# Batch 0 through quadrant scores, a seven-product first stage in the last unit, and a new order of all steps

## The chip, the cores and the metric

The kernel runs on one core of a Trainium2 chip. The metric is the device time of one execution in microseconds (us); the median of several runs counts. One further execution was recorded by the hardware profiler, and all durations come from that one. The engines are PE (TensorE), DVE (VectorE), ACT (ScalarE), POOL (GpSimd) and SP (SyncE, which here only issues DMAs).

## What is computed

Eight batches of attention with pooled keys and values, followed by an MLP mixer over the 576 tokens and the 512 channels:

```python
def _attn_ref(q, k, v):                      # 8 batches, 8 heads, 576 tokens, 64 wide
    k_p = k.reshape(B, H, Sp, 8, D).mean(axis=3)     # 72 pooled keys
    v_p = v.reshape(B, H, Sp, 8, D).mean(axis=3)
    scores = scale * np.matmul(q, k_p.transpose(0, 1, 3, 2))
    attn = softmax(scores)
    return np.matmul(attn, v_p)

def _moe_ref(x, w_tok1, w_tok2, w_ch1, w_ch2):       # x: 8 x 576 x 512
    xt = x.transpose(0, 2, 1)
    h = np.maximum(xt @ w_tok1, 0.0) @ w_tok2        # 576 -> 256 -> 576
    u = x + h.transpose(0, 2, 1)
    h2 = np.maximum(u @ w_ch1, 0.0) @ w_ch2          # 512 -> 1536 -> 512
    return u + h2
```

(The lines are shortened; the softmax subtracts the row's maximum.) Inputs and output are fp32; the kernel multiplies in bf16 and adds up in fp32.

## The kernel before

**Units.** The channel MLP is cut into nine units of 512 rows: unit n (0 to 7) takes tokens 0 to 511 of batch n, and unit 8, the last, takes the remaining 64 tokens of all eight batches. The function `unit_fast` (L574) makes one unit. Its first stage has twelve tiles (`l1_tile`, L514): each is four matmuls of 512 columns with a weight of `w_ch1`, summed in one PSUM bank (L517), and one relu by ACT into the tile `GT` (L521). Its second stage is seven half products of twelve matmuls of 256 columns (L583), after Strassen's scheme in Winograd's form: DVE makes sums of parts of GT (`g_sums`, steps "=1" to "=4", L545 and L557, into the tile called area) and of `w_ch2` (`weight_sum`, steps w0 to w3, made once, area2), and adds up the products (L626, tiles s1, s5, s4, oa and ob, called s and o in the profile). In units 0 to 7 the products come in the order x, y, z, x again, w, z again, x again. In the last unit w is left out and the product is put behind as a seventh on x; x lies there in two PSUM tiles of `ps_two`, called p in the profile. A product that adds to a bank has to wait until DVE has read the bank's earlier state.

**Steps of a batch.** What turns q, k and v of a batch into a unit's input is a set of named steps (`batch_steps`, L187): loads (lk, lq, lv), pooling of k and v by eights (K0, K1, V0, V1 on POOL and k0, k1, v0, v1 on DVE, all by `pool8`, L171, three additions for half the heads; kpool and vpool0, vpool1 on PE, eight matmuls with the identity each), kpT (the pooled k transposed into kD), Q0 and Q1 (q transposed in 32 by 32 blocks by DVE into qD, L284), s0 to s2 (scores and exponentials), av0 to av4 (attention times values and division by the sum, L379 to L384), at0 and at1 (first token matmul and relu), u0 to u4 (second token matmul and residual, L415), t0 to t3 (transposition by PE) or M0 to M4, M, MT and T0 to T5 (the same through HBM, by SP's DMAs and DVE).

**Order.** The program order is written by hand. `HEAD` (L21) lists the steps before unit 0, and `PLAN` (L22) has one entry for each unit: after the unit's i-th piece (two matmuls of a first-stage tile, or four of a product), the steps under i are issued. Each engine runs its instructions in that order. The step g (`gate`, L711) makes POOL wait for what DVE has before it. Four single PSUM banks (p1a to p1d) are handed out in turn (`take`, `give`), and two double tiles (p) serve scores and attention.

**The head.** Batch 0 goes its own way. Two fp32 transfers by SP bring the first half of q (into qf, which lies in area2), cast by ACT and DVE (steps c0, c1); the other half, k and v come by POOL's converting transfers (`first_kv`, L130, parts A, B and T: first heads, second heads, last eight rows). q is transposed by PE (`qT`, five transposes a step, q0 to q3), k is pooled by PE (`kp2`, kp0 to kp2) and transposed by PE with zeros beside it (`kt2`), and each score step (o0 to o3, e0 to e3, L318) makes the scores of one pair of heads, odd or even tokens. Attention times values comes in halves of the heads (a00 to a14, L333), the token matmuls too (m00 to m14, L356), and the unit's input is made transposed at once (X0 to X3 and A0 to A3, L468 and L476). The steps d1, d2 and so on are spare matmuls on a zeroed tile, 19 in all (L679).

Of the kernel before, what the change touches and what calls it, by code (L numbers as in the profile page):

```python
# [8 lines left out]
FP32 = mybir.dt.float32  # L9
BF16 = mybir.dt.bfloat16  # L10
# [10 lines left out]
HEAD = """LkA LkT LkB LvT Lq LvA LvB Lt1 Lk1 Lt2 Lc1b Lc1a Lq1 Lc1c Lv1 Lc1d p1 Lc2a Lc2b Lc2c d2 d2 d3 d1 d4 d4 c0 c1 prep q0 kp0 kp1 kt0 q1 d1 o0 kt1 kp2 e0 e1 q3 kt2 o1 q2 e3 vpool0 o3 e2 a00 vpool1 a02 o2 m01 d1 d1 m00 a04 X1 m03 a14 m02 X0 m04 p0 a10 a12 1.kpool m10 m14 m12 m13 m11 A1 A0 X2 X3 A2 A3"""  # L21
PLAN = [  # L22
# [13 lines left out]
def kernel(  # L36
# [18 lines left out]
    BOUNCED = range(3, B)  # L55
    SP = S // POOL
    BP, BR = 64, S // 64
    NE = (BR + 1) // 2
    EV, OD = NE * BP, (BR - NE) * BP
# [35 lines left out]
    GT = singles.tile([P, NM, 4 * P], BF16)  # L95
    area2 = early.tile([P, 6 * 1024], BF16, name="area2")
    qf = area2[:, 0:4 * BR * D].bitcast(FP32).rearrange("p (a n) -> p a n", a=2)
    f2 = area2[:, 2304:2304 + 2 * S].rearrange("p (c n) -> p c n", c=2)
    warm = area2[:, 3584:4096]
    uT_tails = singles.tile([P, 4, 4 * P], BF16)  # L100
    u_tails = singles.tile([P, 2, DM, 2], BF16)
    area = early.tile([P, 6 * 1024], BF16, name="area")
    kpz = area[0:SP, 0:1536].rearrange("j (h e d) -> j h e d", h=H, e=3)
    kT = area[:, 2048:2048 + 2 * H * SP].rearrange("m (o k) -> m o k", o=2)
    qT0 = area[:, 3200:3200 + 2 * HP * EV].rearrange("m (a l n) -> m a l n", a=HP, l=2)
# [3 lines left out]
    exps = [singles.tile([SP, H * S + BP], BF16, name=f"ex{i}") for i in range(2)]  # L109
# [20 lines left out]
    def first_kv(key, part):  # L130
        if (0, key) not in loaded:
            loaded[0, key] = raw.tile([SP, H, POOL, D], BF16, name=key + "r")
        h0, h1, j0, j1 = {"A": (0, HP, 0, BP), "B": (HP, H, 0, BP), "T": (0, H, BP, SP)}[part]
        kv(loaded[0, key], k if key == "k" else v, 0, h0, h1, j0, j1)

    def q_pairs(a0, a1):
        return q[0, 2 * a0:2 * a1].rearrange("(a l) (p r) d -> (l p) a (r d)", l=2, r=BR)
# [49 lines left out]
    def batch_steps(b):  # L187
# [5 lines left out]
        def prepare():  # L193
            kp = att.tile([SP, 2, 2, 4, D // 2], BF16, name="kp") if b >= 1 else None
            st.update(kp=kp, vp=values[par], ex=exps[par], xt=rests[b // 2 % 2])
            if not first:
                st["kD"] = att.tile([P, 2, 2, SP], BF16, name="kD")
# [29 lines left out]
        def kp2(h0, h1):  # L227
            def go():
                ps = take([P, 512], FP32)
                n = (h1 - h0) * D  # L230
                for i in range(POOL):
                    nc.tensor.matmul(out=ps[0:SP, 0:n], lhsT=ident[0:SP, 0:SP], rhs=loaded[b, "k"][:, h0:h1, i, :],
                                     start=(i == 0), stop=(i == POOL - 1))
                nc.vector.tensor_copy(out=kpz[:, h0:h1, 1, :], in_=ps[0:SP, 0:n].rearrange("j (h d) -> j h d", d=D))
                give(ps)
            return go

        def kt2(h0, h1):
            def go():
                ps = take([P, 2, h1 - h0, SP], BF16)  # L240
                for odd in range(2):
                    for h in range(h0, h1):
                        nc.tensor.transpose(out=ps[:, odd, h - h0, :],
                                            in_=kpz[:, h, 1 - odd:3 - odd].rearrange("j e d -> j (e d)"),
                                            identity=ident[0:SP, 0:SP])
                nc.vector.tensor_copy(out=kT[:, :, h0 * SP:h1 * SP], in_=ps.rearrange("m o h j -> m o (h j)"))
                give(ps)
            return go
# [22 lines left out]
        def qT(hp):  # L271
            def go():
                ps = take([P, NE, 2, BP], BF16)
                for rr in range(NE):
                    nc.tensor.transpose(out=ps[:, rr].rearrange("m l p -> m (l p)"),
                                        in_=loaded[b, "q"][:, hp, rr * P:(rr + 1) * P], identity=ident)
                nc.vector.tensor_copy(out=qT0[:, hp].rearrange("m l (r p) -> m r l p", p=BP), in_=ps)
                give(ps)
            return go

# [8 lines left out]
        def scores(i):  # L289
            def go():  # L290
                pss = [ps_two.tile([P, 2, 512], FP32, name="p2") for _ in range(2)]
                spans = [(i, 0, 0, S1)] if i < 2 else [(g, g * (S - S1), S1, S) for g in range(2)]
                for g, o, n0, n1 in spans:
                    for db in range(2):
                        for l in range(4):
                            quad = slice(l * 32, (l + 1) * 32)
                            nc.tensor.matmul(out=pss[l // 2][0:SP, l % 2, o:o + n1 - n0], lhsT=st["kD"][quad, g, db, :],  # L297
# [3 lines left out]
                for a in range(2):  # L301
                    if i < 2:
                        dst, src = exv[:, a, :, i, 0:S1], pss[a][0:SP, :, 0:S1]
                    else:
                        dst, src = exv[:, a, :, :, S1:S], pss[a][0:SP, :, 0:2 * (S - S1)].rearrange("j l (g n) -> j l g n", g=2)
                    nc.scalar.activation(out=dst, in_=src, func=AF.Exp, scale=scale)  # L306
            return go

        def score(hp, odd):
            n = OD if odd else EV  # L310

            def go():
# [470 lines left out]
```

## Time and profile before

| | |
|---|---|
| Runs | 265.97 us median of 3 (265.03 to 266.37) |
| Profiled execution, span | 264.4 us |
| PE busy | 256.2 us, 2121 matmuls |
| DVE, ACT, POOL busy | 178.4, 119.6, 153.1 us |
| First matmul of unit 0, of unit 8 | 24.60 us, 240.72 us |
| Last unit: first product, last product | 251.09 us, 259.42 us |
| Granted clock of PE, mean | 0.999 |

The span runs from the first to the last instruction of the profiled execution; the time of a run also holds what lies around it. A matmul's row shows its whole passage, 0.379 us for 512 columns, while the next one starts 0.216 us after it, so that many matmuls in a row are read from their starts.

### The profile page before, as it was taken

How to read it: one execution, taken by the hardware profiler on the slowest of the kernel's cores; microseconds unless marked ns; L12 is line 12 of the kernel's file. 1: busy time of each engine (PE TensorE's matmuls, PEld its weight loads, DVE VectorE, ACT ScalarE, POOL GpSimd, SP SyncE). 2: the span in 40 equal slices, each digit the busy share in tenths (PEclk: the TensorE clock that was granted, in tenths of full speed). 3: DMA queues.
4: the chain of work that ended last, by engine and by line, in shares of the span. 5: the costliest groups of instructions: out<-in, count | busy, mean ns of one | idle time of the engine just before them, and what ended most of it. 6: DMA issues, size and time to landing. Idle time of an engine off the chain costs nothing.

```text
span 264.4 us, 5328 instructions
## 1 busy us (share of the span) xinstructions
PE 256.2 (97%) x2121; PEld 160.3 (61%) x2121; DVE 178.4 (67%) x370; ACT 119.6 (45%) x195; POOL 153.1 (58%) x177
## 2 busy tenths in 40 slices
PE   8799999989999999999999999999999999999994
PEld 3685466744677545774487447744874486486483
DVE  3557569996787655895599678844795576184183
ACT  2355763149536456425641575165435412612700
POOL 8577326899999999988959982898200010100000
PEclk9999999999999999999999999999999999999999
DMA  6999999993088928699447940830513053404104
GB/s 141 193 195 206 205 207 208 205 216 80 4 129 141 166 82 171 149 202 266 91 132 107 232 144 17 158 94 4 159 38 122 30 170 80 121 0 102 59 0 159
DMA packets 31704, 34.29 MB, mean 130 GB/s; under 512 B 3136, under 2 KB 23744, under 8 KB 31680
## 3 DMA queue, kind: packets, MB, share of 16 engines
q0 software_dynamic: 17632, 17.64, 42.3%
q1 hardware_dynamic: 13632, 15.93, 20.2%
q10 hardware_dynamic: 416, 0.39, 0.5%
q8 instruction: 16, 0.26, 0.4%
q14 instruction: 8, 0.07, 0.1%
HBM read 38.99 MB, written 12.58 MB: 195 GB/s over the span
## 4 chain that ended last, share of the span: by engine, by line
PE 73%; DVE 12%; POOL 8%; issue 3%; DMA 2%; ACT 1%; POOLq 0%; ACTq 0%
PE p1c L517 10%; PE p1b L517 8%; PE p1a L517 7%; PE p1d L517 7%; PE p1d L583 6%; PE p1c L583 5%; PE p1b L583 4%; PE p1a L583 4%; POOL t L174 3%; PE p L297 3%; DVE x L384 3%; DVE area L545 3%; PE p L379 2%; DMA kr<-in_k_dram 2%; POOL t L175 2%
## 5 line engine op out<-in xcount | busy, mean ns | idle before, releaser
L517 PEld LDWEIGHTS <-w_ch 128*128 128x128 bf16 x432 | 39.5, 98 | 44.4 <-issue 2.7
L713 POOL COPY flag<-flag 1x1 f32<-1x1 f32 x47 | 15.3, 326 | 86.0 <-DVE flag L712 86.0
L583 PEld LDWEIGHTS <-area 128*128 128x128 bf16 x432 | 41.4, 98 | 7.8 <-issue 1.2
L306 ACT ACTIVATE ex<-p 72x768 bf16<-72x768 f32 x42 | 31.6, 803 | 17.1 <-PE p L297 17.1
L583 PEld LDWEIGHTS <-GT 128*128 128x128 bf16 x324 | 30.7, 98 | 7.9 <-issue 1.6
L175 POOL TENSOR_TENSOR t<-t 72x512 f32<-72x512 f32 x23 | 31.2, 1358 | 1.8
L517 PE MATMUL p1c<-uT,w_ch 128*128 128x512 bf16 x116 | 31.4, 379 | 0.0
L521 ACT ACTIVATE GT<-p1b 128x512 bf16<-128x512 f32 x27 | 16.1, 597 | 27.5 <-PE p1b L517 20.9
L521 ACT ACTIVATE GT<-p1c 128x512 bf16<-128x512 f32 x32 | 19.1, 598 | 15.5 <-PE p1c L517 11.7
L517 PE MATMUL p1b<-uT,w_ch 128*128 128x512 bf16 x96 | 26.0, 379 | 0.0
L174 POOL TENSOR_TENSOR t<-kr 72x1024 f32<-72x1024 bf16 x12 | 25.5, 2121 | 0.4
L174 POOL TENSOR_TENSOR t<-vr 72x1024 f32<-72x1024 bf16 x11 | 23.4, 2125 | 1.0 <-DMA vr<-in_v_dram 0.5
L517 PE MATMUL p1a<-uT,w_ch 128*128 128x512 bf16 x88 | 23.9, 379 | 0.0
L517 PE MATMUL p1d<-uT,w_ch 128*128 128x512 bf16 x84 | 22.2, 379 | 0.0
L521 ACT ACTIVATE GT<-p1a 128x512 bf16<-128x512 f32 x25 | 14.9, 597 | 15.4 <-PE p1a L517 14.8
L521 ACT ACTIVATE GT<-p1d 128x512 bf16<-128x512 f32 x24 | 14.4, 599 | 12.8 <-PE p1d L517 7.3
L384 DVE TENSOR_TENSOR x<-p,den 128x512 bf16<-128x512 f32 x28 | 19.3, 691 | 1.0
L545 DVE TENSOR_TENSOR area<-GT 128x1536 bf16<-128x1536 bf16 x9 | 11.3, 1257 | 11.9 <-ACT GT L521 6.7
L557 DVE TENSOR_TENSOR area<-GT 128x1536 bf16<-128x1536 bf16 x9 | 9.5, 1054 | 11.3 <-ACT GT L521 11.3
L379 PEld LDWEIGHTS <-ex 72*128 72x128 bf16 x280 | 12.9, 98 | 6.5 <-DVE x L384 1.4
L379 PE MATMUL p<-vp,ex 72*128 72x65 bf16 x280 | 14.4, 194 | 0.3 <-POOL vp L180 0.2
L118 POOL DMA_DIRECT2D kr<-in_k_dram x17 | 10.9, 646 | 5.6 <-PE p1b L222 1.9
(185 smaller groups left out, 464.2 us busy)
## 6 DMA issues: line engine op xcount, KB each, us to landing
out_dram<-o SPq DMA_DIRECT2D x32, 256.0 KB, 4.2
qb<-in_q_dram POOLq DMA_DIRECT2D x7, 576.0 KB, 9.4
kr<-in_k_dram POOLq DMA_DIRECT2D x7, 512.0 KB, 8.4
vr<-in_v_dram POOLq DMA_DIRECT2D x7, 512.0 KB, 14.0
w_ch<-in_moe_w_ch_dram POOLq DMA_DIRECT2D x5, 512.0 KB, 14.8
mem<-u SPq DMA_DIRECT2D x10, 256.0 KB, 2.2
v<-mem SPq DMA_DIRECT2D x20, 128.0 KB, 2.9
area<-in_q_dram SPq DMA_DIRECT2D x2, 288.0 KB, 3.0
```

The costliest lines, as they stand in the source:

```text
L118: nc.gpsimd.dma_start(out=t[j0:j1, h0:h1].rearrange("j h i d -> j h (i d)"), in_=src[b, h0:h1].rearrange("h (j i) d -> j h (i d)", i=POOL) ...
L174: eng.tensor_tensor(out=t4[:, 0:n], in0=t[:, hs, 0:4], in1=t[:, hs, 4:8], op=ALU.add)
L175: eng.tensor_tensor(out=t4[:, 0:n, 0:2], in0=t4[:, 0:n, 0:2], in1=t4[:, 0:n, 2:4], op=ALU.add)
L306: nc.scalar.activation(out=dst, in_=src, func=AF.Exp, scale=scale)
L379: nc.tensor.matmul(out=ps[:, h // 4, (h % 4) * (D + 1):(h % 4 + 1) * (D + 1)], lhsT=st["ex"][:, h * S + n0:h * S + n0 + P], rhs=st["vp"][: ...
L384: nc.vector.tensor_tensor(out=dst.rearrange("p (a h d) -> p a h d", a=2, d=D), in0=view[:, :, :, 0:D], in1=den[rows, :, :, None].broadcast ...
L517: nc.tensor.matmul(out=ps, lhsT=w_ch1[:, kk, m * P:(m + 1) * P], rhs=uT[kk], start=(kk == 0), stop=(kk == 3))
L521: nc.scalar.activation(out=GT[:, m, :], in_=ps, func=AF.Relu)
L545: nc.vector.tensor_tensor(out=out, in0=a, in1=b, op=ALU.subtract)
L557: nc.vector.tensor_tensor(out=S4[:, 0], in0=GT[:, f, hi], in1=GT[:, sec, hi], op=ALU.add)
L583: nc.tensor.matmul(out=ps[i] if split else ps[:, i], lhsT=chunk(u, i, a(m)), rhs=w(m), start=start and m == 0 and (i == 0 or split), stop= ...
L713: nc.gpsimd.tensor_copy(out=flag[:, 1:2], in_=flag[:, 0:1])
```

## The change

`HEAD` and all of `PLAN` are written anew; the diff below shows the entries for the head, unit 0 and the last three units. Steps that stay keep their meaning.

Batch 0: the first four heads of k come in fp32, by one transfer of SP (64 rows) and one of ACT (8 rows), into `kf` (in area), and DVE pools them (k0). The other four heads are pooled by PE (kp1). q comes by two converting transfers (Lq0, Lq+) in the layout of the later batches, four heads at a time, and DVE transposes it (Q0, Q1). The scores are made in quadrants, in spans of 512 and 64 tokens (S0, S1, S2). The spare matmuls number 22.

Last unit, first stage (`l1_fast`): the weight is cut into two by two parts, and so is the input; seven products of 256 columns take the place of eight. Three groups (A, B, C) of two rows of tiles go through products 1 to 7 in the order of `ORDER`. The sums of weight parts are made by DVE in unit 7 (z0 to z3), those of the input likewise (y0 to y3). ACT copies three intermediate states of each group out of PSUM, DVE adds three times a group and takes the maximum with zero, and ACT makes the fourth output's relu. `GT` now holds its two column halves apart. Batch 1's second half of v is pooled by DVE (v1) instead of by PE, and batch 3's first half of v by PE instead of by POOL.

```diff
-HEAD = """LkA LkT LkB LvT Lq LvA LvB Lt1 Lk1 Lt2 Lc1b Lc1a Lq1 Lc1c Lv1 Lc1d p1 Lc2a Lc2b Lc2c d2 d2 d3 d1 d4 d4 c0 c1 prep q0 kp0 kp1 kt0 q1 d1 o0 kt1 kp2 e0 e1 q3 kt2 o1 q2 e3 vpool0 o3 e2 a00 vpool1 a02 o2 m01 d1 d1 m00 a04 X1 m03 a14 m02 X0 m04 p0 a10 a12 1.kpool m10 m14 m12 m13 m11 A1 A0 X2 X3 A2 A3"""
+HEAD = """LkT LkB Lq0 prep k0 LvT Q0 LvB d3 Lq+ d4 LvA Lt1 d2 Lt2 Lk1 Lc1a d1 Lq1 d4 Lc1b Lc1c Lv1 d3 p1 kt0 Lc1d kp1 S0 d3 kt1 Lc2b d2 Lc2a Q1 vpool1 S2 S1 vpool0 a04 p0 a14 a00 m04 Lc2c a02 m14 a10 m01 X0 a12 m02 m00 m03 m10 X1 m11 m12 A1 m13 X3 A0 1.kpool X2 A2 1.Q1 A3 0.u1 1.kpT 0.u3"""
 PLAN = [
-    {0: "2.lk 0.u1 1.kpT 1.Q0 1.Q1", 3: "0.u0 3.lq 2.lq", 6: "1.s0 0.u2", 8: "g", 9: "0.u3 1.s1", 10: "1.vpool1 2.lv", 12: "1.s2 1.vpool0", 13: "=3", 14: "1.av1 1.av2", 17: "1.av0", 18: "1.av4 g", 19: "w0", 20: "3.lv 1.av3", 22: "w1", 23: "g =1 =2", 24: "3.lk", 25: "=4", 26: "1.at0 g", 27: "2.K0", 28: "w3 1.at1", 30: "g", 31: "1.u2", 32: "2.K1", 33: "1.u0 2.V0", 34: "1.u1", 35: "w2", 37: "1.t2", 40: "1.u3", 41: "1.t0", 42: "1.t3", 43: "1.t1 2.Q0 1.u4", 44: "g 2.kpT 2.Q1 3.Q0"},
+    {0: "1.s1 2.lk 2.lq", 3: "1.Q0 0.u0", 4: "0.u2", 7: "1.s0", 8: "g 1.vpool0 g", 11: "2.lv 1.v1", 12: "1.s2 g", 13: "=3", 14: "1.av2", 15: "1.av1", 17: "1.av4", 18: "1.av0 3.lv 3.lq", 19: "w0", 20: "1.av3", 22: "w1", 23: "1.at1", 24: "3.lk =1 =2", 25: "=4", 26: "g 2.K0", 28: "w3 1.at0", 30: "2.K1 1.u1", 32: "2.V0 1.u0", 33: "g", 35: "w2 1.t0", 37: "1.u2", 40: "1.t2 1.u3", 41: "2.Q1", 42: "1.t3", 43: "2.Q0 1.t1 1.u4"},
...
+    {0: "2.kpT 3.Q0", 2: "2.s0", 6: "2.s2", 7: "3.K1", 8: "2.v1 g", 13: "2.s1", 14: "3.K0", 16: "2.av3", 17: "4.lq", 18: "2.av4", 19: "2.av0 3.Q1 5.lk", 22: "2.av1", 23: "2.av2 =1", 24: "g", 25: "=2", 26: "4.lk g", 28: "2.at0 2.at1", 30: "=4", 31: "3.kpT 2.u3", 32: "3.s2", 33: "2.u2", 34: "2.t3 =3 4.Q1", 36: "3.V1", 37: "3.s0", 38: "3.vpool0", 40: "g 2.u1 3.s1 2.u0", 41: "2.t2", 42: "4.lv 2.t0 g", 43: "2.t1 3.av0", 44: "3.av4"},
...
-    {3: "7.MT", 4: "7.T4", 13: "g", 18: "g", 21: "g", 24: "=3", 25: "=1", 27: "7.T5", 28: "=2", 30: "g", 32: "=4", 42: "g", 43: "g"},
-    {22: "=3", 24: "=1", 25: "g", 26: "=2", 27: "=4", 42: "g"},
+    {8: "z0", 9: "g", 10: "z2 z1", 12: "g", 19: "z3", 22: "=3", 25: "=1", 26: "g", 27: "=2", 29: "7.T4", 30: "7.T5", 33: "=4 8.y0", 37: "8.y2", 39: "8.y1", 41: "8.y3"},
+    {23: "=1", 28: "=2", 30: "=4", 35: "=3"},
 ]
...
-    GT = singles.tile([P, NM, 4 * P], BF16)
+    GT = singles.tile([P, 2, NM, 2 * P], BF16)
...
+    kf = area[0:SP, 0:4096].bitcast(FP32).rearrange("j (l i d) -> j l i d", l=HP, i=POOL)
...
-        def kp2(h0, h1):
+        def kp2(g):
             def go():
                 ps = take([P, 512], FP32)
...
+                    nc.tensor.matmul(out=ps[0:SP, 0:HP * D], lhsT=ident[0:SP, 0:SP], rhs=loaded[b, "k"][:, hs, i, :],
                                      start=(i == 0), stop=(i == POOL - 1))
...
+        def kt2(g):
+            def go():
+                ps = take([P, 2, SP], BF16)
+                for e in range(2):
+                    nc.tensor.transpose(out=ps[:, e, :], in_=st["kp"][:, g, e].rearrange("j l d -> j (l d)"),
+                                        identity=ident[0:SP, 0:SP])
+                nc.vector.tensor_copy(out=st["kD"][:, g], in_=ps)
                 give(ps)
...
-        def scores(i):
+        def scores(spans):
...
+            name[f"s{g}"], name[f"S{g}"], name[f"f{g}"] = (scores([(g, *r)]) for r in ((0, S1), (0, 512), (S1, S)))
+        name["s2"], name["S2"] = (scores([(g, n, S) for g in range(2)]) for n in (S1, 512))
...
+    def ch1_sum(k):
+        a11, a21 = (w_ch1[:, 0:2, i * NH * P:(i + 1) * NH * P] for i in range(2))
+        a12, a22 = (w_ch1[:, 2:4, i * NH * P:(i + 1) * NH * P] for i in range(2))
...
+    def l1_fast(n, uT):
...
+        factors = {1: (w(0, 0), b(0, lo)), 2: (w(0, 1), b(1, lo)), 3: (ws(3), b(1, hi)), 4: (w(1, 1), us(3)),
+                   5: (ws(0), us(0)), 6: (ws(1), us(1)), 7: (ws(2), us(2))}
...
+        def keep(g, k):
+            kept[g, k] = spare[len(kept) % len(spare)]
+            nc.scalar.copy(out=kept[g, k], in_=bank[g, k == 5])
+
+        def add(g, k, ps, row, half):
+            dst = GT[:, half, row * NH + 2 * g:row * NH + 2 * g + 2]
+            nc.vector.tensor_tensor(out=dst, in0=ps, in1=kept[g, k], op=ALU.add)
+            if g > 0:
+                dst = GT[:, half, row * NH + 4 * (g - 1):row * NH + 2 * g + 2]
+                nc.vector.tensor_scalar(out=dst, in0=dst, scalar1=0.0, scalar2=None, op0=ALU.max)
+
+        def step(g, k):
...
+            ps = bank[g, k in (2, 3, 5)]
+            a, c = factors[k]
+            for j in range(2):
+                for kk in range(2):
+                    nc.tensor.matmul(out=ps[:, j], lhsT=a(2 * g + j, kk), rhs=c(kk),
+                                     start=k in (1, 2, 5) and j == 0 and kk == 0, stop=kk == 1, skip_group_check=True)
+            if k == 1 or k == 5:
+                keep(g, k)
+            elif k == 6:
+                keep(g, 2)
+            elif k == 2:
+                add(g, 1, ps, 0, 0)
+            elif k == 3:
+                add(g, 2, ps, 0, 1)
+            elif k == 7:
+                add(g, 5, ps, 1, 1)
+            else:
+                nc.scalar.activation(out=GT[:, 0, NH + 2 * g:NH + 2 * g + 2], in_=ps, func=AF.Relu)
...
+    ORDER = "A1 A2 B1 B2 A6 C1 C2 A5 A7 B6 A3 B5 B7 A4 C6 B3 C5 B4 C7 C3 C4"
...
+        if n in FAST:
+            step = l1_fast(n, uT)
+            for t in ORDER.split():
+                step("ABC".index(t[0]), int(t[1]))
+                yield
...
-        for a in range(2):
-            nc.sync.dma_start(out=qf[:, a:a + 1, :], in_=q_pairs(a, a + 1))
...
+        for j0, j1 in ((0, BP), (BP, SP)):
+            (nc.scalar if j0 else nc.sync).dma_start(out=kf[j0:j1].rearrange("j l i d -> j l (i d)"),
+                                                     in_=k[0, 0:HP].rearrange("h (j i) d -> j h (i d)", i=POOL)[j0:j1])
```

More of the change, by code (lines that the diff above doesn't have):

```diff
@@ L54 @@
     POOL = 8
-    BOUNCED = range(3, B)
+    BOUNCED = [b for b in range(B) if any(f"{b}.M" in t.split() for at in PLAN for t in at.values())]
     SP = S // POOL
     BP, BR = 64, S // 64
-    NE = (BR + 1) // 2
-    EV, OD = NE * BP, (BR - NE) * BP
     S1 = 3 * P
@@ L193, in prepare @@
         def prepare():
[L194 to L197, printed above, removed]
+            st["kp"] = att.tile([SP, 2, 2, 4, D // 2], BF16, name="kp")
+            st["kD"] = att.tile([P, 2, 2, SP], BF16, name="kD")
+            st.update(vp=values[par], ex=exps[par], xt=rests[b // 2 % 2])
         def late(key):
@@ L269, in ppool @@
             return go
[L271 to L279, printed above, removed]
         def qD(g):
@@ new lines, in u_sum, with w, ws, b @@
+    def u_sum(n, k):
+        uT = batches[n][2]["uT"] if n < B else uT_tails
+        b12, b21, b22 = uT[:, 0:2, hi], uT[:, 2:4, lo], uT[:, 2:4, hi]
+        if k == 0:
+            U1[n] = raw.tile([P, 4, 2, 256], BF16, name="qb")
+        t = U1[n]
+        sub(t[:, k], *((b12, uT[:, 0:2, lo]), (b22, t[:, 0]), (b22, b12), (b21, t[:, 1]))[k])
+    def l1_fast(n, uT):
+        def w(i, k):
+            return lambda m, kk: w_ch1[:, 2 * k + kk, (i * NH + m) * P:(i * NH + m + 1) * P]
+        def ws(k):
+            return lambda m, kk: C1[k][:, kk, m * P:(m + 1) * P]
+        def b(k, half):
+            return lambda kk: uT[2 * k + kk][:, half]
+        def us(k):
+            return lambda kk: U1[n][:, k, kk]
+        factors = {1: (w(0, 0), b(0, lo)), 2: (w(0, 1), b(1, lo)), 3: (ws(3), b(1, hi)), 4: (w(1, 1), us(3)),
+                   5: (ws(0), us(0)), 6: (ws(1), us(1)), 7: (ws(2), us(2))}
+        bank, kept = {}, {}
+        def keep(g, k):
[8 more added lines that the diff above has]
+        def step(g, k):
+            if k == 1:
+                if g > 0:
+                    bank[g, 0], bank[g, 1] = (take([P, 2, 256], FP32) for _ in range(2))
+                else:
+                    bank[g, 0], bank[g, 1] = (ps_two.tile([P, 2, 512], FP32, name="p2")[:, 0].rearrange(
+                        "p (j n) -> p j n", j=2) for _ in range(2))
+            ps = bank[g, k in (2, 3, 5)]
[14 more added lines that the diff above has]
+                add(g, 5, ps, 1, 1)
+            else:
+                nc.scalar.activation(out=GT[:, 0, NH + 2 * g:NH + 2 * g + 2], in_=ps, func=AF.Relu)
+                if g == NM // 4 - 1:
+                    for i in range(4):
+                        give(bank[1 + i % 2, i // 2])
+        return step
@@ L576, in unit_fast @@
         uT = [u["uT"][:, kk, :] for kk in range(4)]
-        for m in range(NM):
-            yield from l1_tile(n, m, uT)
+        if n in FAST:
[3 more added lines that the diff above has]
+                yield
+            for _ in range(3):
+                yield
+        else:
+            for m in range(NM):
+                yield from l1_tile(n, m, uT)
         def product(ps, a, w, start, after, split=False, end=None):
@@ L687, in head @@
             batches[1][0]()
-        elif s[0] == "c":
-            a = int(s[1:])
-            (nc.vector.tensor_copy if a % 2 else nc.scalar.copy)(out=loaded[0, "q"][:, a, 0:BR * D], in_=qf[:, a, :])
         else:
@@ L750 @@
             head(s)
-        for n in range(B + 1):
-            unit(n, PLAN[n])
+        for n, at in enumerate(PLAN):
+            unit(n, at)
 _INS = ['q', 'k', 'v', 'moe_w_tok1', 'moe_w_tok2', 'moe_w_ch1', 'moe_w_ch2']
```

107 lines of the change are left out of this document (45 added, 62 removed), and 11 rows, old and new, of the table PLAN.

## The prediction

> **What bounds the kernel now.** I read the page's busy table first, then who waits for whom on PE, then the timeline of the head (0 to 30 us) and of the last unit (from 240.7 us).
>
> ```profile
> PE 256.2 (97%) x2121; PEld 160.3 (61%) x2121; DVE 178.4 (67%) x370; ACT 119.6 (45%) x195; POOL 153.1 (58%) x177
> ...
> PE p1d L232 <- DMA kr<-in_k_dram: 1.3, 1, 1.3
> ...
> PE p1c L222 <- POOL kp L178: 0.9, 1, 0.9
> ```
>
> PE is busy for 97% of the span, and its only long waits are 1.3 us for the first k, 0.9 us for kpT at the end of unit 0, and the 3.5 us after the last matmul. So between the ends a step costs what PE streams for it; only in the head and in the last unit do other chains set the pace. The head:
>
> ```profile
> 8.04 0.61 PE L232 MATMUL p1d<-kr,ident 72*72 72x128 bf16 x8 [1.30 <-DMA kr<-in_k_dram]
> ...
> 15.16 0.41 PE L333 MATMUL p<-vp,ex 72*128 72x65 bf16 x8 [0.41 <-ACT ex L322]
> ...
> 19.60 1.89 PE L253 MATMUL p1b<-kr,ident 72*72 72x512 bf16 x8
> 20.39 0.20 DVE L338 RECIPROCAL den<-p 128x8 f32<-128x8 f32 x1
> 20.62 0.69 DVE L339 TENSOR_TENSOR x<-p,den 128x512 bf16<-128x512 f32 x1
> ...
> 24.60 0.59 PE L517 MATMUL p1c<-uT,w_ch 128*128 128x512 bf16 x2
> ```
>
> k lands, the scores and exponentials fill 8 to 17.6 us, attention times values starts at 15.16 and its DVE divisions end at 21.31; unit 0 starts at 24.60. The last unit:
>
> ```profile
> 250.22 1.03 PE L517 MATMUL p1b<-uT_tails,w_ch 128*128 128x512 bf16 x4
> 251.09 1.47 PE L583 MATMUL p<-w_ch,GT 128*128 128x256 bf16 x12
> ...
> 256.78 1.47 PE L583 MATMUL p1d<-w_ch,area 128*128 128x256 bf16 x12 [0.29 <-DVE s L626]
> 258.09 1.47 PE L583 MATMUL p<-area,area 128*128 128x256 bf16 x12
> ```
>
> Its first stage runs from 240.72 to 251.09 without a gap; then seven products of 1.31 us follow, and one of them waits for DVE already.
>
> **Last unit, work removed.** 48 matmuls of 512 columns, four per 0.864 us (251.09 less 240.72 is 10.37 us for twelve fours), become 21 products of four matmuls of 256 columns; twelve of those take 1.31 us, so a product takes 0.437 and the stage 9.17. Gain on PE: 1.20 us.
>
> **Last unit, work added.** DVE now closes each output. Nine additions from PSUM at 0.68 (as L626, 128x512) are 6.1 us. Six maxima in SBUF (three of 1024 elements, three of 512) have no row. A two-operand bf16 sum of 1536 takes 0.95, and a one-operand fp32 cast (L690, 576 elements) 0.46: both run near 0.53 ns an element beyond a fixed 0.15, half the 1.03 of the PSUM rows. If one operand and bf16 halve it twice, 1024 elements take 0.42 and 512 take 0.29; if once, 0.69 and 0.42; at the PSUM rate 1.2 and 0.68. I take the first, an estimate, since both halvings stand in rows, and keep the others for the range. ACT's twelve copies and relus at 0.60 replace twelve relus and cost nothing.
>
> [...]
>
> Followed in DVE's order, in us from the unit's start: additions for A and B run with PE, C7's comes out at 9.3, and product C4, which accumulates into the bank that C7's addition reads, waits for it: 8.74 becomes 9.3, so the stage ends near 9.8. C3's addition and maximum end at 10.6. Then the queue is: sum "=1" 0.95, two s1 parts 0.7, "=2" 0.95, oa 0.68, "=4" 0.95, s5 0.74: 15.5. Only then may the fifth product add to its bank: 15.6, where before it was 16.06 (256.78). s2 (0.7) and "=3" (0.95, formerly done at 247.7, during the first stage) end at 17.1, and the sixth product starts at 17.2, before at 17.37. So of 1.20 us only about 0.2 arrives: the place of the stall is now DVE's queue. Bounds: with the slow maxima (0.69) +0.7, at the PSUM rate +3; with no queueing -0.85. Taken -0.2. The unit-7 additions (four weight sums of 0.95, four u sums of some 0.42) lie where DVE was idle from 222.8 to 229.6 and in its gaps up to 240; they push unit 7's last additions by 0.8 us into the new unit, whose bank for C2 is needed 2.6 us in: nothing, or 0.3 if that cover is gone.
>
> **Head.** Removed on PE: 20 q transposes (0.44 a five: 1.8 us), 16 of 24 k pooling matmuls, 12 of 16 k transposes, 16 score matmuls of 256 or 320 columns; added: scores in quadrants (eight of 384 columns took 0.47, so some 0.6 for 512) and three spare matmuls (0.22 each). PE has room here, so only the chain counts. The two fp32 transfers of k's first half replace those of q, the same 576 KB; those landed by 4.33. On DVE three adds follow: at the PSUM rate 1.2, 0.68 and 0.42, together 2.3; as DVE did it for v at 59.2, beside POOL, 4.0. Either way they end at 6.7 to 8.4. The half of q that S0 needs is the third software transfer, after 32 and 256 KB of k. By increments of the old landings (issue 1.24 plus 5.4 for the first, 1.3 per 256 KB, 1.1 for 288 KB) it lands at 7.2 to 8.3; by the bytes ahead of it, as the third of before did, at 9.3; I take 8.0. The quadrant transposition (L284, 0.76) ends at 8.85, the kD copy at 9.15, S0 starts at 9.25.
>
> From there, in the order that the diff gives: two exponentials of 1024 (0.82 ns an element more than the 0.59 row of 512: 1.95 the pair) to 11.85; the other q half lands three transfers later, 11.3, transposed at 12.1; S2 and its two small exponentials to 13.55; S1 has to wait for their PSUM tiles, its exponentials end at 16.25; a04 starts at 15.8 and a14 at 16.3. Two tail divisions (0.6) and four full ones (0.9, as 0.20 and 0.69) end at 21.0, where it was 21.31. PE still has six m's behind or beside that, kpool (1.7, now behind the divisions rather than at 19.6), X and A steps, and 0.u1, kpT, 0.u3 (1.0 us, moved ahead of the unit). With no gap unit 0 starts at 25.8, with the gaps for evictions at 26.3. At 26.03 the old kernel had done four matmuls of unit 0 (0.86) and u1, kpT, but not u3 (0.43): I am behind by +0.2 to +0.7, less if q comes early. Taken +0.3; bounds -0.6 and, with q at 9.3 and late exponentials, +1.7.
>
> **Units 0 and 1.** kpT of batch 2 moves behind unit 1's first step, and K1 loses the flag that held it: K0 follows "=4" near 45.6, two poolings of 4.3 end at 54.2, not 57.45. The stall at 57.50 goes, 1.1 us (56.39 to 57.50). What is late next is nothing on PE: the scores wait for qD, transposed before. The pooling of batch 1's v by PE (0.87 us) goes to DVE, and batch 3's comes to PE: zero together. On DVE v1 takes 2.3 to 4.0 us, starting when the v of batch 1 is there (31.2) and vpool0's copy is done, about 33. Behind it wait "=3" and five divisions, and for those av2, which PE reaches at 35.4. At 2.3 PE waits nothing, at 4.0 some 1.3. POOL pools nothing then, so I take the short side and +0.2. Moved loads keep their bytes ahead within 0.3 MB, and every c1 and c2 piece lands before its use; POOL's queue of issues, eight transfers deep, is as full as before. The other moved steps in units 1 to 7 I cost at 0, bounds -2 and +1: PE is seen busy for 182.7 of 183.2 us there, yet the chain holds 3% of "issue" time, so small waits exist.
>
> **Sum.** -0.2 + 0.3 - 1.1 + 0.2 = -0.8. The profiled execution's span is 264.4, which becomes 263.6; the median of the runs is 265.97, 1.6 above it for start and end, which the change leaves: 265.2. Less or more than 0.5% (1.33 us) is about what a measurement of this kernel can tell from no change.
>
> **Rivals.** *The new order sheds small waits* in units 1 to 7 that I set at nothing: a quarter of the 3% of issue time is 2.0 us, 263.2. For it: every step was re-placed, and POOL runs 3 us earlier; against: PE's rows there have hardly a gap. 0.27.
>
> *The q half gates the head*, the slower side. Everything up to a12 hangs on one transposition that waits for one landing. At 9.3 by bytes it costs 1.3 more (266.5); if it takes 7.9 from its issue at 2.6, as the halves of v did, 2.5 more (267.7); together 267.1. It decides from a landing at 8.8 on. For it: the fp32 transfers run in the same time; against: only 288 KB of software traffic is ahead. 0.15.
>
> *The maxima run slowly*: +0.9, 266.1, if 1024 elements take 0.69. 0.04.
>
> *The clock falls back.* In the old head the first ten matmuls of 512 columns started 0.425 apart and the later ones 0.215. From 12.6 to 17 us the new PE has gaps and no spare matmuls; if that lowers the clock once more, some 1.8 us of matmuls take twice as long: 267.0. The old gap of 1.3 us did nothing of the kind. 0.04. [...]
>
> **How the numbers follow.** The forecast case has 0.50 and its own range, 264.2 to 266.2; some 0.15 of it lies beyond -0.5%. Faster: 0.27 + 0.15 = 0.42. Slower: most of the q, clock and maxima cases, 0.21. Same: 0.37. The range for all, 262.8 to 267.8, holds the first rival's middle and the q rival up to its end.
>
> **What would show it.** S0 near 9.3 and its first exponential near 10; a04 near 15.8; last x near 21.0; the first L485 matmul at 25.8 to 26.3; no wait of PE for kp at the end of unit 0; in the last unit a wait of about 0.5 us before C4, then waits for DVE ahead of the fifth and the sixth product, the sixth 17.2 us after the unit's start. It is wrong if the last unit ends much earlier or later against its start, if the L587 rows are not near 0.42, or if the half of q lands outside 7.2 to 9.3.

## The result and the profile after

The changed kernel takes 278.97 us, median of 4 runs (278.39 to 280.53), the kernel before beside it 265.94 us (265.03 to 266.37): a ratio of 1.050, 95% interval 1.046 to 1.054. The span of the profiled execution grows from 264.4 to 277.7 us. The change makes the kernel 13 us slower; 0.8 us faster was forecast.

The busy table of the page, and its rows of PE's busy share and of the granted clock over 40 slices of 6.9 us (tenths):

```profile
PE 259.5 (93%) x2105; PEld 164.5 (59%) x2128; DVE 193.7 (70%) x382; ACT 117.2 (42%) x192; POOL 148.1 (53%) x165
...
PE   7779999999999999919999999999999998999994
...
PEclk9757999999999999986999999999999999999999
```

The same two rows before:

```profile
PE   8799999989999999999999999999999999999994
...
PEclk9999999999999999999999999999999999999999
```

PE's busy share falls from 97% to 93%. Two places differ from before: the first three slices, where PE is 70% busy, with a clock that falls to 0.5 in the third of them, and a slice near 120 us in which PE stands still, again with a lower clock behind it (6 tenths in the next slice). The starts of the units' first matmuls in the timeline of PE, and the spans, in us, tell how much each place costs; the last four columns are runs told of below.

| | before | after | e5 | e7 | e8 | e9 |
|---|---|---|---|---|---|---|
| unit 0 | 24.60 | 30.51 | 27.41 | 28.56 | 26.96 | 26.91 |
| unit 1 | 57.58 | 60.64 | 57.56 | 58.69 | 57.09 | 57.02 |
| unit 2 | 87.64 | 92.09 | 88.14 | 89.26 | 87.66 | 88.43 |
| unit 3 | 115.70 | 127.75 | 116.19 | 117.31 | 115.71 | 117.12 |
| unit 4 | 145.48 | 158.33 | 145.90 | 147.39 | 145.43 | 147.83 |
| unit 8 | 240.72 | 254.45 | 241.14 | 243.07 | 241.13 | 243.16 |
| span | 264.39 | 277.70 | 264.51 | 265.91 | 263.98 | 266.38 |

Unit 0 starts 5.9 us late, unit 0 itself gives back 2.85, unit 1 loses 1.4, unit 2 loses 7.6, the units behind it lose 1.7 in small pieces, and the last unit gives back 0.4.

The head, in the timeline of all engines (start and duration in us, engine, line, operation, idle time before it and what ended that; other rows in between are left out):

```profile
5.56 0.81 PE L735 MATMUL p1b<-area 128*128 128x512 bf16 x3
5.88 1.22 DVE L170 TENSOR_TENSOR t<-area 72x1024 f32<-72x1024 f32 x1 [3.81 <-DMA area<-in_k_dram]
8.34 0.24 PE L238 MATMUL p1c<-ident,kp 72*128 72x72 bf16 x2 [1.97 <-DVE kp L174]
8.86 0.78 DVE L268 STREAM_TRANSPOSE qD<-qb 128x576 uint32<-128x576 uint32 x1 [0.57 <-DMA qb<-in_q_dram]
10.49 1.93 ACT L293 ACTIVATE ex<-p 72x1024 bf16<-72x1024 f32 x2 [7.86 <-PE p L283]
12.28 1.91 PE L258 MATMUL p1d<-vr,ident 72*72 72x256 bf16 x8
18.76 0.62 PE L304 MATMUL p<-vp,ex 72*128 72x65 bf16 x8 [0.52 <-DVE vp L261]
23.80 0.69 DVE L310 TENSOR_TENSOR x<-p,den 128x512 bf16<-128x512 f32 x1
30.51 0.59 PE L485 MATMUL p1b<-uT,w_ch 128*128 128x512 bf16 x2
```

The same stretch by windows: the window and its length, the busy time of PE, its weight loads, DVE, ACT and POOL in us, each with its instructions in brackets, and behind POOL's the granted clock:

```profile
6.40:8.40 2.00, 0.06 (x2) 0.07 (x2) 1.81 (x3) 0.00 (x0) 1.42 (x3) 1.00 1.11 185
8.40:9.40 1.00, 1.00 (x10) 0.81 (x10) 0.54 (x1) 0.00 (x0) 0.47 (x2) 1.00 1.23 206
9.40:10.40 1.00, 0.67 (x10) 0.17 (x10) 0.68 (x3) 0.00 (x0) 0.89 (x2) 1.00 1.18 218
10.40:11.40 1.00, 1.00 (x9) 0.43 (x6) 0.00 (x0) 0.91 (x1) 0.45 (x2) 0.68 1.12 194
...
14.00:18.00 4.00, 3.53 (x33) 1.99 (x32) 0.00 (x0) 2.88 (x6) 4.00 (x6) 0.50 1.24 205
...
26.00:30.00 4.00, 4.00 (x28) 2.22 (x27) 2.40 (x5) 1.16 (x3) 0.71 (x2) 1.00 1.25 204
```

The spare matmuls end near 6.4; PE then waits 1.97 us for DVE's sums of k and works with gaps. From 10.8 to about 24 us the clock is at half (0.50 in 14 to 18 us): eight pooling matmuls take 1.91 us at 12.28, where eight of that form take 1.04 at full clock (e9, at 82.31).

Unit 2, the timeline of PE and DVE at its end, then the DMAs issued in 111 to 113 us (KB each, median us to landing):

```profile
118.13 0.42 PE L350 MATMUL p<-vp,ex 72*128 72x65 bf16 x8
122.54 0.45 DVE L429 STREAM_TRANSPOSE uT<-v 128x256 uint32<-128x256 uint32 x1 [7.44 <-DMA v<-mem]
124.78 1.44 PE L639 MATMUL p1a<-area,area 128*128 128x256 bf16 x6 [6.23 <-DVE flag L768]
```

```profile
qb<-in_q_dram POOLq DMA_DIRECT2D x2, 576.0 KB, 7.7
v<-mem SPq DMA_DIRECT2D x4, 128.0 KB, 6.4
```

and the same in the kernel before, issued in 106 to 108.2 us, where no load is issued beside them:

```profile
v<-mem SPq DMA_DIRECT2D x4, 128.0 KB, 2.8
```

SP's four reads of u (step M) go out at 111.05 to 112.40, POOL's loads of q for batches 5 and 6 at 111.14 and 111.88, and its loads of v from 113.55 on. The reads land at 113.4, 115.6, 120.5 and 122.4. DVE's transposition stands ahead of its sums for the products, so PE's next product, whose bank DVE has not read, waits 6.23 us. The clock falls once more behind that (0.50 in 124.7 to 128 us).

The last unit, on PE and DVE:

```profile
254.45 1.04 PE L600 MATMUL p<-uT_tails,w_ch 128*128 128x256 bf16 x8
...
263.76 0.60 PE L600 MATMUL p1c<-qb,w_ch 128*128 128x256 bf16 x4 [0.40 <-DVE GT L584]
264.19 1.47 PE L639 MATMUL p<-w_ch,GT 128*128 128x256 bf16 x12
...
271.21 1.49 PE L639 MATMUL p<-area,area 128*128 128x256 bf16 x12
```

```profile
261.24 0.43 DVE L587 TENSOR_SCALAR GT<-GT 128x1024 bf16<-128x1024 bf16 x1
...
263.74 0.29 DVE L587 TENSOR_SCALAR GT<-GT 128x512 bf16<-128x512 bf16 x1
```

Its first stage takes 9.74 us (10.37 before), with the wait ahead of C4; the whole unit 23.25 (23.67 before).

### The profile page after: what moved, and what is told of

Same layout as the page of the kernel before. It is cut to its first block, busy times and chain, and to the rows that moved or that the text cites. A ratio compares the mean times of both kernels' runs of the same rounds, so it can differ in the third digit from the quotient of the medians.

```text
span 277.7 us, 5321 instructions
## 1 busy us (share of the span) xinstructions
PE 259.5 (93%) x2105; PEld 164.5 (59%) x2128; DVE 193.7 (70%) x382; ACT 117.2 (42%) x192; POOL 148.1 (53%) x165
## 5 line engine op out<-in xcount | busy, mean ns | idle before, releaser
L485 PEld LDWEIGHTS <-w_ch 128*128 128x128 bf16 x384 | 35.1, 99 | 40.9 <-issue 4.4
L293 ACT ACTIVATE ex<-p 72x768 bf16<-72x768 f32 (+2 forms) x48 | 36.1, 803 | 29.5 <-PE p L283 29.5
L485 PE MATMUL p1c<-uT,w_ch 128*128 128x512 bf16 x96 | 26.5, 384 | 0.3
L485 PE MATMUL p1d<-uT,w_ch 128*128 128x512 bf16 x88 | 24.4, 379 | 0.4 <-issue 0.3
L489 ACT ACTIVATE GT<-p1b 128x512 bf16<-128x512 f32 x25 | 14.9, 598 | 22.7 <-issue 15.5
L489 ACT ACTIVATE GT<-p1c 128x512 bf16<-128x512 f32 x25 | 14.9, 597 | 18.1 <-PE p1c L485 9.8
L170 POOL TENSOR_TENSOR t<-vr 72x1024 f32<-72x1024 bf16 x10 | 21.2, 2122 | 0.4
L489 ACT ACTIVATE GT<-p1a 128x512 bf16<-128x512 f32 x23 | 13.7, 598 | 16.8 <-PE p1a L485 16.7
L513 DVE TENSOR_TENSOR area<-GT 128x1536 bf16<-128x1536 bf16 x9 | 13.4, 1494 | 6.6 <-ACT GT L489 6.6
L525 DVE TENSOR_TENSOR area<-GT 128x1536 bf16<-128x1536 bf16 x9 | 8.9, 986 | 12.1 <-ACT GT L489 12.1
L489 ACT ACTIVATE GT<-p1d 128x512 bf16<-128x512 f32 x23 | 13.7, 597 | 7.1 <-PE p1d L485 7.1
L639 PE MATMUL p1a<-area,area 128*128 128x256 bf16 x72 | 10.4, 297 | 6.2 <-DVE flag L768 6.2
```

Source lines behind the costliest of these rows:

```text
L170: eng.tensor_tensor(out=t4[:, 0:n], in0=t[:, hs, 0:4], in1=t[:, hs, 4:8], op=ALU.add)
L485: nc.tensor.matmul(out=ps, lhsT=w_ch1[:, kk, m * P:(m + 1) * P], rhs=uT[kk], start=(kk == 0), stop=(kk == 3))
L489: nc.scalar.activation(out=GT[:, :, m, :], in_=ps.rearrange("p (h n) -> p h n", h=2), func=AF.Relu)
L513: nc.vector.tensor_tensor(out=out, in0=a, in1=b, op=ALU.subtract)
L525: nc.vector.tensor_tensor(out=S4[:, 0], in0=GT[:, 1, f], in1=GT[:, 1, sec], op=ALU.add)
L639: nc.tensor.matmul(out=ps[i] if split else ps[:, i], lhsT=chunk(u, i, a(m)), rhs=w(m), start=start and m == 0 and (i == 0 or split), stop= ...
```

## The experiments

Two theories stood at the start: *clock* (PE's gaps in the head lower its clock, so spare matmuls bring the time back) and *traffic* (loads beside the reads of u make unit 2 stand still). Each ratio is to the kernel before, run beside it on the same chip, with its 95% interval.

**e1, nine more spare matmuls ahead of kt0.**

```diff
-... Lv1 d3 p1 kt0 ...
+... Lv1 d3 d9 p1 kt0 ...
```

> Nine more spare matmuls before kt0 fill the 2.0 us in which PE was idle (6.4 to 8.3 us). Theory 'clock' (that gap lets the granted clock fall from 10.3 to 24 us, and the half-speed matmuls cost the head 4 to 5 us): clock near 0.99, first matmul of unit 0 near 26 us instead of 30.5, the run 4 to 5 us shorter, near 274.5. Rival 'chain' (the head is late because k, q and the exponentials come late, and the clock only fills slack): unit 0 still at 30, time within 1 us of 279.

278.03 us, 1.041 (1.036 to 1.047). The gap before kt0 is filled and the clock still falls (0.83 in 14 to 18 us, 0.50 in 18 to 22), so that gap was not the only cause. Unit 0 starts at 28.78, 1.7 us earlier, but the nine spares are not shown to do that: e2 and e7 below have the changed kernel's own head, and in their profiles the clock falls at 15.6 and 16.1 us and unit 0 starts at 28.87 and 28.56. When the clock falls differs between executions of the same head. The stall in unit 2 is still 5.94 us.

**e2, the loads of unit 2 behind the reads.**

```diff
-26: "5.lq", ... 29: "4.s1 6.lq g", 30: "3.M 5.lv", 31: "g =4", ... 33: "4.av1"
+... 29: "4.s1 g", 30: "3.M", 31: "=4", ... 33: "4.av1 g 5.lq 6.lq 5.lv"
```

> In unit 2 the loads of q5, q6 and v5 are put behind step 3.T3, so that they start after the four reads of u from HBM have landed. Theory 'traffic' (the q loads, issued at the same time as those reads, stretch them from 2.8 to 6.4 us and up to 10, and DVE and then PE stand still): reads at 2.4 to 3.0 us, no PE wait of 6.2 us at 118 us, no fall of the clock behind it, 7 to 8 us less, near 271.5. Rival 'late sum' (the sum =3 beside POOL's pooling took 3.82 us and pushed u and the spill back; the order itself does not fit): the wait stays at 4 us or more, time within 2 us of 279.

275.11 us, 1.031 (1.025 to 1.037). The stall is gone: unit 2's second stage takes 11.1 us as before. But v of batch 5 now lands late and PE waits 2.2 us for its pooling in unit 3, so only 1.9%, 5 us, came back. (This edit moves the two loads of q and that of v together; b3 below moves the loads of q alone.)

**e3, both edits.**

> Both edits. If the two losses are separate and the only large ones: 12 us less than the changed kernel, 266 to 267.5, level with the kernel before. If they overlap, or the head is slow for another reason, 270 or more.

274.41 us, 1.029 (1.023 to 1.035): no different from e2. The clock still fell in the head (at 16.7 us), and once more at 143 us behind the wait of 2.2 us in unit 3 (0.94 on the mean of 140 to 170 us).

**e4, e3 with 16 further spares between kp1 and a14.**

```diff
-kp1 S0 d3 kt1 Lc2b d2 Lc2a Q1 vpool1 S2 S1 vpool0 a04 p0 a14
+kp1 d2 S0 d3 kt1 Lc2b d4 Lc2a Q1 vpool1 d4 S2 d3 S1 vpool0 d3 a04 p0 d2 a14
```

> As both edits, with 16 more spare matmuls spread over the later gaps of the head (before S0, kt1, S2, S1, a04, a14). If the clock falls again in those gaps (half speed after 12 us), 1 to 3 us less than with both edits. If the first gap alone decides, the clock is full already and the spares lie in the way: 0.5 to 2 us more.

272.41 us, 1.021 (1.017 to 1.025). The clock is 1.00 in every window of the head from its rise at 6.0 us on, and unit 0 starts at 28.19. So with spare matmuls in the later gaps the clock stays up, and the head is 3.6 us late even so (1.0 us of that are u1, kpT and u3, moved ahead of unit 0).

**e5 and e7, the old order in units 1 to 6.** e7 is the changed kernel with the old entries of PLAN for these units (kpT of batch 2 stays behind unit 1's first step); e5 has the spares of e4 too, 25 more than the changed kernel (the text put on record for it says 28).

> The changed kernel with units 1 to 6 in the old order, and its own head with no further spare matmuls: what is left against the run with the old order and 28 spares is the clock in the head alone. Theory 'clock in the head is worth 3 us, and the new order of units 1 to 6 the rest': the granted clock falls between 10 and 25 us, unit 0 starts about 5 to 6 us late, units 1 to 6 take their old time with no wait over 1 us, 269.5 to 271.5. Rival 'a late head makes the stall in unit 2': the wait for the reads of u comes back with 5 us of lateness, 273 or more.

> The changed kernel with the 28 more spare matmuls in the head, and with units 1 to 6 in the old order (the old entries of PLAN; only kpT of batch 2 stays behind unit 1's first step, as in the change). Theory 'the new order' (the reads of u share their time with loads only because these were re-placed): no wait of more than 1 us in units 1 to 6, each of them takes its old time, the second unit starts some 0.75 us late and the last unit gives back 0.4, so 266.0 to 267.0. Rival 'late start' (a head that ends late pushes the sums and reads into the loads whatever the order): the wait of 2 us or more in unit 2 or 3 comes back, 269 or more.

e7: 267.86 us, 1.0075 (1.0045 to 1.0104). e5: 267.53, 1.0034 (1.0019 to 1.0049). e7 is 1.6 us under what was expected of it, e5 0.5 us over. Each of units 1 to 6 takes its old time to within about half a microsecond (unit 1 holds kpT now), although e7's unit 0 starts 4.0 us late: a late head doesn't make the stall. The new order of units 1 to 6 costs 4.2% (1.050 less 1.0075), 11 us by the runs. In the two profiles these units differ by 9.4 us (174.3 against 164.8); another 2.0 us lie in the head, whose clock fell at 10.8 us in one profile and at 16.1 in the other, so by the runs the 11 us hold some of that too. With the later fall, the clock in the head is worth 0.4% of e7, 1.1 us (e7 less e5; unit 0 starts 1.15 us apart).

**b3, the same traffic in the kernel before.** Only the two loads of q are moved, ahead of POOL's pooling of v:

```diff
-23: "4.V0 g", ... 26: "5.lq 4.s0", ... 29: "=4 6.lq"
+23: "5.lq 6.lq 4.V0 g", ... 26: "4.s0", ... 29: "=4"
```

> The kernel before, with nothing of the change; only the two loads of q in unit 2 (batches 5 and 6) stand ahead of POOL's pooling of v, so that they are under way when the reads of u start at 106. Theory 'traffic': the four reads land 4 to 10 us after their issue instead of 2.4 to 3.0, PE waits 2 to 5 us for them at the end of unit 2, 268 to 271. Rival 'late sum' (in the changed kernel the reads were late because their data was): the reads land nearly as before, and the time is within 1 us of the kernel before.

269.39 us, 1.012 (1.009 to 1.016): 3.3 us slower, with nothing of the change. The DMAs issued in 106 to 108.2 us, and the wait of PE:

```profile
v<-mem SPq DMA_DIRECT2D x4, 128.0 KB, 6.8
```

```profile
114.65 0.77 DVE L458 STREAM_TRANSPOSE uT<-v 128x256 uint32<-128x256 uint32 x2 [2.03 <-DMA v<-mem]
116.05 1.03 PE L583 MATMUL p1d<-area,area 128*128 128x256 bf16 x8 [1.90 <-DVE flag L712]
```

It is the chain of the changed kernel. The wait is shorter, and a little under what was expected: the reads are issued 3 us behind the loads of q here, the loads of v follow 4.3 us behind the first read instead of 2.5, and the slowest read takes 6.9 us instead of 10.0. Unit 2 is 2.4 us longer than before (30.46 for 28.06).

**e6 and e8, the head.** e6 is e5 with the half of q for S0 as the first software transfer; e8 is e6 with S0 ahead of kp1 and 11 spares fewer (the text put on record for it says 8). The diff goes from e5 to e8; e6 has only the first of its edits, Lq0 in front.

```diff
-LkT LkB Lq0 prep k0 ... d3 d9 p1 kt0 Lc1d kp1 d2 S0 d3 kt1 Lc2b d4 Lc2a Q1 vpool1 d4 S2 d3 S1 ...
+Lq0 LkT LkB prep k0 ... d3 d6 p1 kt0 Lc1d S0 kp1 d2 kt1 Lc2b d2 Lc2a Q1 vpool1 d2 S2 d2 S1 ...
```

> The same, and the half of q that the first scores need is issued as the first software transfer instead of the third. Theory 'the q half gates the head': it lands near 7 instead of 9.4, S0 starts near 9.3 instead of 10.6 (then gated by k's sums on DVE), unit 0 starts 0.6 to 1.2 us earlier, and the time is 265.0 to 266.2. Rival 'exponentials and the second q half': S0 is earlier, but the second half of q or the last exponentials set the end as before, unit 0 moves by less than 0.3 us, and the time is that of the kernel beside it.

> The run with q first, with S0 ahead of the pooling of k's second half on PE, and 8 fewer spares. Theory 'the q half and what PE's queue has ahead of S0 gate the head': S0 starts at 9.2 to 9.6 instead of 9.84 to 10.97, unit 0 starts at 26.2 to 27.0, and the time is 265.2 to 266.3. Rival 'the chain of exponentials and divisions is as long as that': unit 0 at 27.4 or later, 267 or more; if the clock falls again for want of spares, 268 or more.

e6: 266.99 us, 1.0024 (1.0008 to 1.0040), no different from e5. q lands at 6.84 instead of 8.38, but S0 starts at 10.97, later than before: the clock rose at 6.7 instead of 3.8 us in this profile, so the spares lasted until 9.5, and the pooling of k's second half stands ahead of S0 on PE. e8 takes both away (its clock rises at 6.5): S0 at 9.33, unit 0 at 26.96, 265.43 us, 0.9967 (0.9945 to 0.9989). Everything that lay ahead of S0 on PE's queue gated the head, once q was early.

```profile
8.77 0.23 PE L238 MATMUL p1d<-ident,kp 72*128 72x72 bf16 x2
9.33 0.65 PE L283 MATMUL p<-qD,kD 32*72 32x512 bf16 x8 [0.33 <-DVE kD L240]
9.90 1.06 PE L227 MATMUL p1a<-kr,ident 72*72 72x256 bf16 x8
```

(timeline of PE in e8: the scores no longer wait behind L227.)

**b1 and b2, the gains alone.** b1 is the kernel before with the change's last unit; b2 has besides no flag before K1 of batch 2, and its kpT behind unit 1's first step. The diff shows b1's edit of PLAN:

```diff
-    {3: "7.MT", 4: "7.T4", 13: "g", ...},
-    {22: "=3", 24: "=1", 25: "g", 26: "=2", 27: "=4", 42: "g"},
+    {3: "7.MT", 8: "z0", 9: "g", 10: "z2 z1", ...},
+    {23: "=1", 28: "=2", 30: "=4", 35: "=3"},
```

> The kernel before, with the change's last unit alone (seven half products, sums in unit 7; MT of batch 7 stays where it was). Theory 'the last unit is worth what the changed kernel shows': its stage 1 takes 9.7 instead of 10.4 us and all of it 0.4 less, so 265.5 (ratio 0.998). Rival 'the sums of weights and input cost something in unit 7': unit 7 gets longer by 0.3 or more, and the time is 265.9 or more.

> The same, and in unit 0 the flag before K1 of batch 2 is gone and kpT of batch 2 stands behind unit 1's first step, as in the change. Theory 'the stall was free to remove': the wait of 0.9 us at the end of unit 0 is gone and nothing takes its place, 264.4 (ratio 0.994). Rival 'the wait moves': POOL's K1 beside DVE's sums slows one of them, and PE waits as long in unit 1; 265.2 or more.

b1: 265.59 us, 0.9973 (0.9956 to 0.9990), where 265.5 was expected. b2: 265.69, 0.9975 (0.9956 to 0.9993), where 264.4 was: the second edit brings nothing. In its profile K0 still starts at 47.53 (45.6 was forecast), K1 follows it at once, its last addition ends at 57.2 instead of 57.45, and kpT waits for it 0.65 us. Taking the flag away is not enough; in the changed kernel other steps around it had been moved as well.

**e9, the new order without the collision.** e8 with the change's own units 1 to 6, except that q of batch 5 is loaded before the pooling of v, and q of batch 6 and v of batch 5 behind the first transposed piece of u. Its head, e8's, has 14 spares more than the changed kernel's (the text put on record for it says 20).

> The run with the repaired head (q first, S0 ahead of the second half of k, 20 spares more than the changed kernel), with the change's own order in units 1 to 6 except the loads of unit 2: q of batch 5 is loaded before the pooling of v instead of beside the reads of u, q of batch 6 and v of batch 5 behind the first transposed piece of u. Theory 'the loads beside the reads are all that is wrong with the new order': the reads land in 2.4 to 3.0 us, no wait over 1 us in units 2 and 3, and the time is that of the same head with the old order, 265 to 267. Rival 'the new order has no room for these loads': v of batch 5 lands after 128, PE waits 2 us or more for its pooling in unit 3, 268 or more. Rival of the prediction 'the new order sheds small waits': 264 or less.

268.40 us, 1.0084 (1.0055 to 1.0113): the time of the second case, without its mechanism, and the third falls. The reads land in 2.5 to 3.0 us, v of batch 5 before 127, and PE has no wait over 1 us, yet unit 1 is 0.84 us longer than in e8, unit 2 0.64, unit 3 0.99. The new order is 3.1 us dearer by the runs (1.0084 less 0.9967) and 2.1 us in units 1 to 6 of the profiles, even without the collision. Two of the three places are seen. In unit 1 it is work and not order: PE pools batch 3's first half of v, eight matmuls that the old order leaves to POOL.

```profile
82.31 1.04 PE L258 MATMUL p1b<-vr,ident 72*72 72x256 bf16 x8
```

In unit 2 it is a wait of PE for a u, behind DVE's sum "=3":

```profile
96.45 4.53 DVE L513 TENSOR_TENSOR area<-GT 128x1536 bf16<-128x1536 bf16 x1 [2.49 <-ACT GT L489]
100.91 0.77 DVE L268 STREAM_TRANSPOSE qD<-qb 128x576 uint32<-128x576 uint32 x1
101.60 0.68 DVE L387 TENSOR_TENSOR u<-p1a,x 128x512 bf16<-128x512 f32 x1
```

```profile
102.33 0.59 PE L485 MATMUL p1a<-uT,w_ch 128*128 128x512 bf16 x2 [0.65 <-DVE u L387]
```

The same sum in the kernel before and in the changed one:

```profile
95.07 2.00 DVE L545 TENSOR_TENSOR area<-GT 128x1536 bf16<-128x1536 bf16 x1 [1.26 <-ACT GT L521]
```

```profile
100.12 3.82 DVE L513 TENSOR_TENSOR area<-GT 128x1536 bf16<-128x1536 bf16 x1 [2.50 <-ACT GT L489]
```

In all three the sum runs while POOL pools, and the u's queue behind it. Unit 3 has only small waits, none above 0.4 us; what they hang on was not tried.

Put together, if these parts add: of the 5.0%, the collision and its wake are 4.2 less 1.2, or 3.0% (8 us; 7.7 in the profiles, units 1 to 6 of the changed kernel less those of e9), the rest of the new order 1.2% (3 us), and the head with its clock 1.1% (3 us, e7 against e8). What is left in e8 is 0.3% the other way. There the late head, the shorter unit 0 and the longer unit 1 come to nothing together (unit 2 starts at 87.66, before at 87.64), so it is about the gain of the last unit, as in b1.

## Why the prediction was wrong, step by step

**"Moved loads keep their bytes ahead ... every c1 and c2 piece lands before its use", and "the other moved steps in units 1 to 7 I cost at 0, bounds -2 and +1".** This is the step that failed: in place of 0, with a bound of +1, these steps cost 11 us by the runs and 9.4 by the profiles. It asked of each moved load whether its own data comes in time, and not which other transfers share that time. The loads of q did land in time; the reads of u beside them did not. The two bounds came from PE's rows of before, where these steps were hidden; what hid them was the order that the change gave up. b3 shows the cause alone, e7 and e9 its size: some 8 us for the collision and its wake. The other 2 to 3 us are the pooling of batch 3's v by PE (0.84 us, which the prediction had set off against batch 1's), a u behind a slow sum (0.64), and small waits that stay unexplained.

**"The clock falls back", 0.04 and 267.0.** The rival held, and the place named (12.6 to 17 us, gaps and no spare matmuls) was nearly right: in the profile the fall lasted from 10.8 to 24 us. Its dismissal was wrong: that a gap of 1.3 us had done nothing before. The longest single idle time behind the first matmul was 1.97 us, in e7 1.05, and the clock fell in both. The fall began at 10.8 us here and at 16.1 in e7, with the same head; the times between changes of the clock in the heads of the changed kernel, e1, e2, e3 and e7 were about 6.8, 10.2 or 13.7 us. What sets the moment of the fall was not shown. The late fall is worth 1.1 us (e7 against e5), below the 1.8 that the rival had. The early one seems to cost more: of the changed kernel's four runs the two with a mean clock of 0.962 (the profiled one) and 0.963 take 279.5 and 280.5 us, the two with 0.973 and 0.975 take 278.5 and 278.4; where in the other three the clock was low is not on record.

**Head, "+0.3", unit 0 at 25.8 to 26.3.** At full clock it starts at 27.41 (e5). The short price of k's sums was right (done at 8.3), the pair of exponentials too (1.93 for 1.95). Two landings were wrong. That of k was taken from two transfers of q of 288 KB each that came by 4.33; the one of 512 KB took until 5.78, and PE stood idle until k's sums were done. The half of q came at 8.4 to 10.2 in the seven profiles with this order of loads, for 8.0; the q rival, which decides from 8.8, was met in six of them. In the changed kernel's own profile q lands at 8.83 and S0 waits for it: transposed by 9.64, kD copied behind that, S0 at 9.81 instead of 9.25. In e5 q lands at 8.38, and S0 starts at 9.84 behind kp1 and two spares; the last full division ends at 22.0 instead of 21.0, and from there to unit 0 lie 5.4 us of PE work, for 4.8 to 5.3. Even e8, with q at 7, reaches only 26.96.

**Units 0 and 1, "-1.1 + 0.2".** Right in the changed kernel: the stall at the end of unit 0 is gone, and unit 0 is 2.85 us shorter; the prediction's parts for it give 2.8 (1.1 for the stall, 1.0 moved into the head, 0.87 of pooling, less 0.2). The 0.87 comes back in unit 1, with batch 3's pooling. And b2 shows that the removed flag was not the reason by itself.

**Last unit, "-0.2".** Right: -0.42 here, -0.30 to -0.83 in the profiles of e5, e7, e8, e9 and b1, with each step in its place. The maxima took 0.43 and 0.29 for 0.42 and 0.29, the wait before C4 is about half a microsecond, and the sixth product starts 16.8 us after the unit's start, for 17.2 (17.37 before). Alone it is worth 0.3% of the runs (b1, 0.1 to 0.4).

**The first rival, "the new order sheds small waits".** False: e9 shows it adding 2 to 3 us.

## What to carry to other kernels

In a tight hand-written order the transfers are placed as well as the instructions: for each load that a change moves, look up which short reads are in flight then, and what is queued behind the instruction that waits for them. In a stage with many gaps of PE, look at the granted clock of several executions, and not only at the longest gap: here the clock stayed up with spare matmuls in every gap (mean of a run 0.997 to 1.000 in e5, 0.985 to 0.987 in e7, whose head has fewer), with those in the first gap alone it did not (e1, 0.50 in 18 to 22 us), and each spare also stands ahead of the matmul that the chain needs. Split a change that bundles several edits: the new last unit alone, or with the repaired head under the old order, is 0.3% faster than the kernel before, where the whole is 5% slower.

## What the runs showed of the hardware

- Four reads of 128 KB from HBM by SP, in packets of about 0.5 KB (393 packets for 0.19 MB in 106 to 108.2 us of the kernel before), took a median of 2.8 us there, where no load is issued beside them, 6.4 us in the changed kernel beside two converting loads of 576 KB (loads of v follow while the last two reads are under way) and 6.8 us in b3, where those two loads began 3 us earlier; the slowest of them took 10.0 us, in the changed kernel. How the reads and the loads share the time was not shown.
- The granted clock fell from 1.00 to 0.50 where PE had no idle time of 2 us (longest 1.97 us in the changed kernel, 1.05 in e7), and neither the longest gap nor PE's busy share just before tells alone when. In the kernel before PE is busy for 2.14 of 3.40 us, with a gap of 1.3, and the clock stays at 1.00; in e1 it is busy for 2.40 of 3.40, with no gap above 0.52, after 6.8 us without one, and the clock falls to 0.50 at the end. What differs is the kind of matmul too: spares and transposes of q there, scores, pooling and attention times values here. Which of it counts stays open.

```profile
4.60:8.00 3.40, 2.14 (x14) 1.02 (x12) 0.71 (x2) 0.00 (x0) 2.97 (x5) 1.00 1.01 145
8.00:11.40 3.40, 3.35 (x43) 2.98 (x44) 1.81 (x6) 0.59 (x1) 1.76 (x3) 1.00 1.24 196
```

```profile
13.30:16.70 3.40, 2.40 (x38) 1.37 (x28) 0.43 (x2) 2.78 (x5) 2.41 (x4) 1.00 1.27 199
16.70:18.00 1.30, 0.95 (x13) 0.73 (x13) 1.09 (x4) 0.87 (x1) 1.30 (x3) 0.50 1.28 217
```

(windows of the kernel before, then of e1.) When the clock rises at the start also varies between executions, from 3.8 to 6.7 us after the span's start with the same spares (e5, e6), and moves what stands behind the spares by a microsecond (the transposition of kp from 8.34 to 9.50).
- A bf16 sum of 1536 elements by DVE took 0.95 us while POOL added nothing (kernel before, at 236.46) and 2.00, 3.82 and 4.53 us where it ran beside POOL's additions in the three orders (kernel before, changed kernel, e9). The meeting alone doesn't settle it: at 105.50 in the kernel before such a sum took 0.96 us beside an addition that took 1.88.
